# First channel product as seven half products, the second one's weights converted early and parked in device memory, and all places in the order set anew

## The chip, the cores and the metric

The kernel runs on one core of one Trainium2 chip. The metric is the device time of one execution in microseconds (us), lower is better. A core has five engines that run beside each other and meet only at semaphores: TensorE (PE in the profile, with its weight loads PEld), VectorE (DVE), ScalarE (ACT), GpSimd (POOL) and SyncE (SP), which here only issues transfers.

## The reference, cut to what matters

Three layers follow each other, for 2 batches of 448 tokens and a width of 768 (12 heads of 64):

```python
scores = cap * tanh(q @ k.T / 8 / cap)                  # attention, 24 heads
x = softmax(scores) @ v
h = gelu(x @ w_in); u, v = halves(h)                    # gated layer, 1024 wide
v_s = w_sg @ (layernorm(v) * g_ln) + b_sg
x = x + (u * v_s) @ w_out
u = x + (relu(x.T @ w_tok1) @ w_tok2).T                 # token mixing
out = u + relu(u @ w_ch1) @ w_ch2                       # channel mixing: 768 -> 1536 -> 768
```

The weights of the last two layers arrive as float64, so that each has to be narrowed to float32 on the chip. To keep float32 accuracy most products are made of three products of a high part and a rest (`hi*hi + hi*lo + lo*hi`): every operand is first split in two.

## The kernel before

Every piece of work is recorded as an operation (`Plan.op`) with the engines that could do it, a cost for each, a key and the tiles it reads and writes. `Plan.schedule` (a list scheduler in the file) then goes through time and gives each engine, among the operations whose inputs are ready and whose buffers are free, the one with the lowest key; the program is written out in the order of the planned starts. An engine runs its instructions in that order and waits where an input is not there. Buffers come from small pools by tag (`BUFS`: 20 of `a`, 13 of `h`, 6 each of `x`, `v`, `q`, 3 each of the narrowing's `r` and `t`, 4 banks `gm` and 2 double banks `sc` for the results of TensorE).

- **Attention** (`attention_all`): 12 pairs of heads. For each there are score blocks (L605, L618, into `sc`), tanh and exp on ACT (L576, L585), values (L631, L648), sums over the keys (L686) and the division (L703 to L717). A score block needs one of the two `sc` banks, which tanh frees.
- **Gated layer and token mixing**: `v_unit`, `u_unit`, `sg_unit`, `out_unit`, `tr_unit`, `tok1_unit`, `tok2_unit`. Their products are all issued in L330. `v_unit` and `u_unit` of the first batch also fill TensorE between the score blocks of the later pairs. `tok2_unit` leaves `u` as a whole tile (L1067), parks it in device memory (`kept`) and splits it (`x`).
- **First channel product, ch1** (`ch1_unit`): 12 column blocks `f`. For each there are 6 weight chunks and 3 terms over all 896 tokens: 36 products, 448 columns wide in the first two blocks, 512 and 384 in the other ten. One relu on ACT (L1098, 896 wide) drains a block into `q` or `a`.
- **Second channel product, ch2** (`ch2_all`, L1179): seven half products in place of eight. The 2 by 2 blocks of the weights (`a11` to `a22`, 128 by 384 for each of 6 `j`) and of the tokens are combined by sums. Some of these run on DVE (L1105, `change`), some as transfers that add to their target (L1160, `gather`, issued by POOL). DVE adds the results up (L1195, `onto`). Each half product is 54 products of TensorE.
- **Narrowing** (`narrow`): a raw tile `r` arrives; ACT scales it (L472) and makes two partial results (L484, L498), DVE joins them (L506). `split` then makes the high part (L417 on ACT, L418 on DVE, L422 on POOL) and the rest (L434 on DVE, L435 on POOL).

Of the kernel before, what the change touches and what calls it, by code (L numbers as in the profile page):

```python
# [18 lines left out]
DM = H * D  # L19
# [6 lines left out]
NR = 3  # L26
# [6 lines left out]
AHEAD, PACE = 62, 2.2  # L33
# [22 lines left out]
}  # L56
W_ON = {
# [17 lines left out]
    "ch2": (74, 5),  # L75
# [4 lines left out]
TURN, STAY = 200.0, 250.0  # L80
TABLE = 1290.0
EARLY = 72.0
KQ = 1.2
HALVES = ("win_u", "wsg", "wout", "tok1", "tok2", "ch1", "ch2")
# [183 lines left out]
class Net:  # L268
# [184 lines left out]
    def narrow(self, src, n, t, key, name, after=None, sign=1.0):  # L453
# [5 lines left out]
        else:  # L459
# [7 lines left out]
            if after:  # L467

                o.deps += after
            self.act(  # L470
                n,
                lambda: nc.scalar.activation(  # L472
                    raw[:, :, 1].bitcast(F32), raw[:, :, 1].bitcast(F32), AF.Copy, scale=2.0**-112
                ),
                [raw],
                [raw],
                130,
                key=key,
            )
# [181 lines left out]
    def sums(self, E, A, key, level, odd):  # L661
# [65 lines left out]
    def attention_all(self):  # L727
        xs = []
        old = None
        for n in range(B * NP + 1):  # L730
            k0 = 10.0 * n
            odd = n % 2 == 1
            if n < B * NP:
# [8 lines left out]
                for j in range(3):  # L742
                    sc = self.scores(qk, j, k0 + 0.4 * j)
                    self.weigh(sc, 2, E[j], k0 + 0.4 * j)
                if not odd:
                    sc = self.scores_rest(qks, k0 + KQ)
                    self.weigh(sc, 2, Q, k0 + KQ)
            if old:
                was = odd == 0
                oqk, oE, oA, oqks, oAs = old  # L750
                self.values(oqk, oE, oA[0], [0, 1], k0 - 2, was)
                self.values(oqk, oE, oA[0], [2], k0 + 2, was)
                if not was:
                    self.values_rest(oqks, oE[3], oAs, k0 + 2.1)
                self.sums(oE, oA[1], k0 + 2.5, LEVEL[n - 1], was)
# [302 lines left out]
    def tok2_unit(self, b, h1, w2, x2, d, kept):  # L1058
# [10 lines left out]
        u = self.x_part(d, b)  # L1069
        self.split(S, lambda: u[:, 0], lambda: u[:, 1], lambda: z.ap, [z], [u])  # L1070
        return u


    def ch1_unit(self, ws, U, f):

        nc = self.nc
        ps = self.bank2()
        even = f < 2
        for m, ts in enumerate((slice(0, S), slice(S, 2 * S)) if even else WIDE):
            terms = []  # L1080
            for d in range(ND):
# [381 lines left out]
```

## Time and profile before

| | us |
|---|---|
| median of 3 runs | 402.62 (402.31 to 403.66) |
| the profiled execution, its own time | 402.18 |
| its span from the first to the last instruction | 400.4 |
| TensorE busy within the span | 391.8 |
| VectorE, ScalarE, GpSimd busy | 292.5, 271.9, 83.9 |

The span is 1.8 us shorter than the execution's own time; that part lies around the program. TensorE's products are pipelined: a product's record lasts longer than the distance to the next one, so the work of a stage is read as the time from its first product's start to that of the next stage, divided by their number, and not as a sum of records. For DVE and ACT the busy time of a stretch divided by its count of instructions is used in the same way.

### The profile page before, as it was taken

Reading aid. Unit: us, or ns where it says so; the run is one execution under the profiler, and the core shown is the slowest. Engines: PE = TensorE matmul, PEld = TensorE weight load, DVE = VectorE, ACT = ScalarE, POOL = GpSimd, SP = SyncE. Lnnn points to the kernel's source line nnn. Section 1 sums busy time; section 2 is a strip of 40 time slices with the busy share of each in tenths; the row PEclk is TensorE's granted clock in tenths of the full one; section 3 lists DMA queues with packets and bytes.
Section 4 is the critical chain, followed back from the end, with each engine's and each line's share of the span. In section 5 each row is a group of like instructions: output and inputs, shape, how many; then the busy total and the mean of one; then the engine's idle time right before and its main releaser. Section 6 shows DMA issues by size and latency. Waiting matters only on the chain. (4 is left out here: it accounts for less than half of the span.)

```text
span 400.4 us, 5874 instructions
## 1 busy us (share of the span) xinstructions
PE 391.8 (98%) x2102; PEld 302.5 (76%) x2102; DVE 292.5 (73%) x503; ACT 271.9 (68%) x438; POOL 83.9 (21%) x96
## 2 busy tenths in 40 slices
PE   8999989999999999999999999999999999999995
PEld 4222224565567899999999998988989999999995
DVE  1799999999557869976379983435466389978871
ACT  6999999999693577365168868776667675542330
POOL 1112140000001425753000100003222141156300
PEclk9999999999999999999999999999999999999999
DMA  7975243444000114043005774558867794364112
GB/s 240 393 276 199 80 178 109 166 133 144 16 1 10 45 54 144 2 155 107 2 0 153 255 225 157 175 180 201 186 166 178 207 300 76 99 115 70 71 71 75
DMA packets 22934, 54.18 MB, mean 135 GB/s; under 512 B 2800, under 2 KB 11632, under 8 KB 22896
## 3 DMA queue, kind: packets, MB, share of 16 engines
q1 hardware_dynamic: 19008, 48.23, 37.0%
q0 software_dynamic: 3744, 5.38, 8.0%
q8 instruction: 18, 0.29, 0.3%
q14 instruction: 20, 0.16, 0.1%
q10 hardware_dynamic: 144, 0.11, 0.1%
HBM read 42.83 MB, written 5.51 MB: 121 GB/s over the span
## 5 line engine op out<-in xcount | busy, mean ns | idle before, releaser
L330 PE MATMUL sc<-x,a 128*128 128x384 f32 (+2 forms) x432 | 87.7, 364 | 0.0
L330 PEld LDWEIGHTS sc<-x,a 128*128 128x128 f32 x432 | 78.8, 188 | 8.8
L1179 PE MATMUL gm<-a,a 128*128 128x448 f32 x252 | 54.7, 367 | 0.0
L1179 PEld LDWEIGHTS gm<-a,a 128*128 128x128 f32 x252 | 47.3, 188 | 4.3
L330 PE MATMUL gm<-a,a 128*128 128x448 f32 (+1 forms) x232 | 46.3, 356 | 0.0
L472 ACT ACTIVATE r<-r 128x512 f32<-128x512 f32 (+2 forms) x64 | 40.8, 644 | 6.6 <-DMA r<-ch_in 6.5
L585 ACT ACTIVATE a<-a,acap 128x896 f32<-128x896 f32 x42 | 43.7, 1096 | 0.1
L330 PEld LDWEIGHTS gm<-a,a 128*128 128x128 f32 x232 | 42.0, 188 | 2.2
L576 ACT ACTIVATE a<-sc,qs 128x896 f32<-128x896 f32 x42 | 42.0, 1057 | 1.8 <-DVE a L667 0.9
L506 DVE SCALAR_TENSOR_TENSOR t<-r,t 128x512 int32<-128x512 int32 (+1 forms) x34 | 25.4, 753 | 23.6 <-ACT t L498 22.1
L435 POOL TENSOR_TENSOR a<-t,a 128x512 fp32r<-128x512 f32 x12 | 18.9, 1575 | 98.9 <-DVE a L418 72.1
L330 PE MATMUL gm<-q,a 128*128 128x448 f32 x160 | 33.0, 366 | 0.0
L605 PE MATMUL sc<-q 64*64 64x448 f32 x264 | 30.0, 552 | 2.2 <-ACT a L576 2.2
L330 PEld LDWEIGHTS gm<-q,a 128*128 128x128 f32 x160 | 30.0, 188 | 2.6
L631 PE MATMUL gm<-a,v 128*64 128x448 f32 x144 | 30.9, 548 | 0.0
L330 PEld LDWEIGHTS gm<-x,a 128*128 128x128 f32 x144 | 26.7, 188 | 4.9 <-DVE v L418 1.4
L330 PE MATMUL gm<-x,a 128*128 128x448 f32 x144 | 30.5, 368 | 0.0
L484 ACT ACTIVATE t<-r 128x512 uint16<-128x512 uint16 (+1 forms) x34 | 27.3, 806 | 2.7 <-DVE a L434 2.0
L1179 PE MATMUL sc<-a,a 128*128 128x448 f32 x126 | 28.9, 367 | 0.0
L656 DVE TENSOR_TENSOR a<-a,a 128x896 f32<-128x896 f32 (+1 forms) x24 | 26.9, 1122 | 1.9 <-ACT a L585 1.6
L498 ACT ACTIVATE t<-r 128x512 f16<-128x512 f32 (+1 forms) x34 | 27.1, 803 | 0.0
L330 PE MATMUL gm<-a,x 128*128 128x512 f32 x108 | 26.5, 397 | 0.0
(130 smaller groups left out, 578.8 us busy)
## 6 DMA issues: line engine op xcount, KB each, us to landing
r<-ch_in SPq DMA_DIRECT2D x18, 512.0 KB, 3.5
r<-ch_in SPq DMA_DIRECT2D x24, 384.0 KB, 3.8
r<-w_in_in SPq DMA_DIRECT2D x12, 512.0 KB, 5.1
q<-qk_in SPq DMA_DIRECT2D x11, 448.0 KB, 7.2
v<-va_in SPq DMA_DIRECT2D x12, 256.0 KB, 6.0
r<-w_out_in SPq DMA_DIRECT2D x6, 512.0 KB, 3.4
u<-h SPq DMA_DIRECT2D x12, 224.0 KB, 2.5
x<-u SPq DMA_DIRECT2D x12, 224.0 KB, 5.9
```

The costliest lines, as they stand in the source:

```text
L330: self.nc.tensor.matmul(view(), l, rr, start=(i + m == 0), stop=(i + m == n - 1))
L435: "POOL": ("POOL", n * 2.3 + 60, lambda: nc.gpsimd.tensor_tensor(**args()), True),
L472: lambda: nc.scalar.activation(raw[:, :, 1].bitcast(F32), raw[:, :, 1].bitcast(F32), AF.Copy, scale=2.0**-112),
L484: lambda: nc.scalar.activation(t.ap.bitcast(U16)[:, 0::2], raw.ap.rearrange("p n t -> p (n t)").bitcast(U16)[:, 1::4], AF.Copy, scale=2.0* ...
L498: lambda: nc.scalar.activation(t.ap.bitcast(F16)[:, 1::2], raw[:, :, 1].bitcast(F32), AF.Copy, scale=sign),
L506: lambda: nc.vector.scalar_tensor_tensor(out=t.ap.bitcast(I32), in0=raw[:, :, 1], scalar=3, in1=t.ap.bitcast(I32), op0=ALU.logical_shift_l ...
L576: lambda: nc.scalar.activation(te.ap, sc[:, 0:nn, :S], AF.Tanh, scale=self.qs),
L585: lambda: nc.scalar.activation(te.ap, te.ap, AF.Exp, scale=self.acap),
L605: nc.tensor.matmul(sc[at, h, :S], part(rows, ks), part(rows, QC), start=True, stop=True)
L631: nc.tensor.matmul(A[cols, :S], V[:, 2 * j + h], E[j][:, h], start=(j == 0 and not odd), stop=(j == 2 and odd),)
L656: "DVE": ("DVE", n / 0.96 + 70, lambda: nc.vector.tensor_tensor(**args()), True),
L1179: nc.tensor.matmul(banks[i].ap[:, :S], l, r, start=not more and (j, n) == (0, 0), stop=(j, n) == (KH - 1, 2), skip_group_check=more,)
```

## The change

1. ch1 becomes `ch1_all`, with the same scheme of seven half products as ch2. The tokens are combined once (for each of three `d` a difference, a sum, two negations and two gathers); there are 21 splits of token tiles in place of 12. For each of 6 `j` the weights come as four 128 by 384 blocks, are combined by three gathers and one sum, and give seven half products of 9 products, all 448 columns wide. Each is split on its own (42 splits of 384 columns in place of 18 of 512). Two of the seven results are drained by ACT, five by an `onto` on DVE, and three relus run on tiles outside the banks.
2. The 24 weight blocks of ch2 are narrowed before ch1 starts, written to device memory (`ahead`), and read back shortly before ch2 (`fetch`).
3. ch2's arithmetic is as before. `a21` and `a22` share tiles of the pool `a`; a gather is planned with fewer bytes.
4. All places are set anew: `off(kind, n, j)` shifts the keys of attention, normalisation, weights, ch1 and the parked blocks by a table, and a few constants change. The scheduler itself does not.

```diff
-AHEAD, PACE = 62, 2.2
+AHEAD, PACE = (36, 10), 2.2
+SCALE_ON = {"ch1": {"ACT": 0, "POOL": 200}, "ch2": {"ACT": 0, "POOL": 200}}
+CH1_ORDER = [(0, 0), (0, 1), (1, 0), (0, 2), (1, 1), (1, 2)]
+for j in range(6):
+    CH1_ORDER += [(p, j) for p in ((2, 3, 5, 4, 6) if j < 3 else (0, 2, 3, 1, 5, 4, 6))]
-    "ch2": (74, 5),
+    "ahead": (-130, 4.2),
-TURN, STAY = 200.0, 250.0
+TURN, STAY = 200.0, 267.5
-EARLY = 72.0
-KQ = 1.2
+EARLY = 72.96
+KQ = 1.42
+OFF = {
+    "a": {
+        (0, 0): 6.9, (0, 1): -3.7, (0, 2): -1.1, (1, 0): 6.2, (1, 1): 27.0, (1, 2): 12.6, (1, 3): 6.6,
...
+    "s": {
+        (0, 0): 2.0, (0, 2): 1.8, (0, 3): 4.5, (1, 0): -1.8, (1, 1): -4.1, (1, 2): 4.3, (2, 0): 5.9,
...
+def off(kind, n, j):
+    return OFF.get(kind, {}).get((n, j), 0.0)
...
-                    sc = self.scores(qk, j, k0 + 0.4 * j)
-                    self.weigh(sc, 2, E[j], k0 + 0.4 * j)
+                    at = k0 + 0.4 * j + off("s", n, j)
+                    sc = self.scores(qk, j, at)
+                    self.weigh(sc, 2, E[j], at)
...
+    def ahead(self, src, n, at, name, sign):
+        t, out = self.buf("t", [128, n]), Buf("keep", None, None)
+        out.ap = self.dram.tile([128, n], F32, tag=name, name=name, bufs=1)
+        self.narrow(src, n, t, at, "ahead", sign=sign)
+        self.load(128 * n * 4, lambda: self.nc.sync.dma_start(out=out.ap, in_=t.ap), [out], [t], key=at)
+        return out
+    def gather(self, out, a, n, at):
+        nc = self.nc
+        self.plan.op(
+            [("POOL", 1000.0, lambda: nc.gpsimd.dma_start(out=out.ap, in_=a.ap, accum_op=ALU.add), False, 0)],
+            at,
+            [a, out],
+            [out],
+            nbytes=205 * n * 4,
+        )
...
+            self.change(z11[d], z11[d], z12[d], ALU.subtract, S, lead(2, 0))
+            o22[d] = self.operand(z22[d], lead(2, 0) + 0.12)
+            self.negate(z12[d], lead(2, 0) + 0.1)
+            self.gather(z12[d], kept[1][3 + d], S, lead(2, 0) + 0.12)
+            self.change(z22[d], z22[d], z11[d], ALU.add, S, lead(2, 0) + 0.17)
...
+            product(0, j, x, a11, o11, False)
+            self.act(S, lambda x=x, o=c12: nc.scalar.copy(o.ap, x.ap[:, :S]), [x], [c12], 60, key=at[0, j])
+            product(1, j, x, a12, o21, True)
+            self.act(S, lambda x=x, o=c11: nc.scalar.activation(o.ap, x.ap[:, :S], AF.Relu), [x], [c11], 60, key=at[1, j])
+            self.gather(a11, a21, 384, at[2, j] - 18 + off("g", 0, j))
+            self.change(s2, a22, a11, ALU.add, 384, at[2, j] - 13 + off("g", 1, j))
+            product(2, j, y, s2, o2, False)
+            self.onto(c12, y, c12, at[2, j], ALU.subtract)
+            self.gather(a12, s2, 384, at[2, j] - 12 + off("g", 2, j))
+            product(3, j, z, a11, o3, False)
+            self.onto(c22, z, c12, at[3, j])
+            product(4, j, z, a22, o4, True)
+            self.onto(c21, z, c12, at[4, j])
+            self.relu(c21, at[4, j])
+            self.gather(a21, a22, 384, at[5, j] - 14 + off("g", 3, j))
+            product(5, j, v, a21, o1, False)
+            self.onto(c22, v, c22, at[5, j])
+            self.relu(c22, at[5, j])
+            product(6, j, v, a12, o22, True)
+            self.onto(c12, v, c12, at[6, j])
+            self.relu(c12, at[6, j])
...
-                narrow(t, row, col, j, k - AHEAD + (4 * j + n) * PACE)
+                self.fetch(t, f32[j, row, col], 128 * 384 * 4, k - AHEAD[n // 2] + (2 * j + n % 2) * PACE)
```

Three places show how the order moves. A row names the line, the instruction, what it writes and what it reads; `x3` means three in a row. L330, L605, L618, L631, L648, L686 and L1160 of before are L404, L675, L688, L701, L718, L756 and L1167 of the change; ch1's products stand in L1239, the POOL casts of L422 in L496.

TensorE in attention, before, at score blocks 25 to 28: `sc` are score blocks, `gm` collect values or sums, `q` holds queries and keys, `a` the exponentials, `v` the values of a pair.

```order
L631 MATMUL gm_9_468<-a_31_485,v_6_174 64x448 x2
L631 MATMUL gm_9_468<-a_32_490,v_6_174 64x448 x2
L605 MATMUL sc_25_527<-q_6_176 64x448 x4
L618 MATMUL sc_26_537<-q_6_176 64x448 x2
L618 MATMUL sc_26_537<-q_7_232 64x448 x2
L605 MATMUL sc_27_550<-q_7_232 64x448 x4
L605 MATMUL sc_28_560<-q_7_232 64x448 x4
L686 MATMUL gm_11_568<-a_30_477,ones_72 64x448 x2
```

The same score blocks of TensorE in the change.

```order
L701 MATMUL gm_10_500<-a_32_505,v_6_193 64x448 x2
L688 MATMUL sc_25_551<-q_6_195 64x448 x2
L688 MATMUL sc_25_551<-q_7_262 64x448 x2
L675 MATMUL sc_26_560<-q_5_191 64x448 x4
L701 MATMUL gm_12_571<-a_34_537,v_7_254 64x448 x2
L701 MATMUL gm_12_571<-a_35_545,v_7_254 64x448 x2
L701 MATMUL gm_12_571<-a_30_479,v_7_254 64x448 x2
L675 MATMUL sc_27_589<-q_7_262 64x448 x4
L675 MATMUL sc_28_596<-q_7_262 64x448 x4
L718 MATMUL gm_12_571<-a_36_574,v_7_254 64x448 x2
```

Before, four score blocks stand in a row, with two banks `sc`; in the change three values blocks stand between score blocks 26 and 27.

TensorE in ch1, before, in the third column block: `x_7` to `x_12` are the split tokens of both batches, `a_119` and `a_121` weights.

```order
L330 MATMUL sc_53_2368<-x_11_2168,a_121_2074 128x512 x3
L330 MATMUL sc_53_2368<-x_12_2179,a_121_2074 128x512 x3
L330 MATMUL sc_53_2368<-x_7_2110,a_119_2061 128x384 x3
L330 MATMUL sc_53_2368<-x_8_2123,a_119_2061 128x384 x3
L330 MATMUL sc_53_2368<-x_9_2129,a_119_2061 128x384 x3
```

ch1 at its start in the change: `gm_80` to `gm_82` are the banks of the first two half products, `x_10` the split tokens of the second.

```order
L1239 MATMUL gm_80_2463<-x_7_2314,a_112_2182 128x448 x3
L1239 MATMUL gm_80_2463<-x_8_2322,a_112_2182 128x448 x3
L1239 MATMUL gm_80_2463<-x_9_2351,a_112_2182 128x448 x3
L1239 MATMUL gm_81_2485<-x_7_2314,a_116_2243 128x448 x3
L1239 MATMUL gm_81_2485<-x_8_2322,a_116_2243 128x448 x3
L1239 MATMUL gm_81_2485<-x_9_2351,a_116_2243 128x448 x3
L1239 MATMUL gm_80_2463<-x_10_2355,a_118_2265 128x448 x3
```

Before, all rows write one bank `sc` and read split tokens; now nine products of 448 columns make one half product of one `j` in a bank `gm`, and the first two half products start in turn. ch1 has 378 products in place of 432.

POOL in ch1, before: the DMA rows are gathers for ch2, the TENSOR_SCALAR rows high parts.

```order
L422 TENSOR_SCALAR a_139_2717<-q_19_2377 128x448
L1160 DMA h_62_2465<-h_63_2487 128x384
L1160 DMA v_27_2549<-h_64_2604 128x384
L422 TENSOR_SCALAR a_143_2796<-q_20_2438 128x448
L1160 DMA h_64_2604<-h_65_2630 128x384
L422 TENSOR_SCALAR a_145_2836<-v_28_2713 128x384
L1160 DMA v_28_2713<-h_66_2770 128x384
```

POOL late in ch1 in the change: `h_76` to `h_79` are the four weight blocks of `j` = 4, `t_55` and `t_56` sums of blocks, `a_172` and `v_31`, `v_32` blocks of ch2.

```order
L496 TENSOR_SCALAR a_167_3096<-h_78_3069 128x384
L1167 DMA h_78_3069<-h_77_3032 128x384
L1167 DMA h_77_3032<-h_79_3101 128x384
L1167 DMA h_76_3013<-t_56_3140 128x384
L1167 DMA v_31_2521<-a_172_3150 128x384
L1167 DMA a_172_3150<-a_172_3150 128x384
L1167 DMA v_32_2575<-a_179_3238 128x384
```

There are 50 gathers in place of 26, and here six stand in a row, ch1's and ch2's behind each other.

## Rows read from the trace of the kernel before

**Rows 1.** The page's head and its first part, busy time of each engine.

```profile
span 400.4 us, 5874 instructions
PE 391.8 (98%) x2102; PEld 302.5 (76%) x2102; DVE 292.5 (73%) x503; ACT 271.9 (68%) x438; POOL 83.9 (21%) x96
```

**Rows 2.** Busy time by stretch: engine busy us (instructions), granted clock, DMA share, GB/s.

```profile
core 0: us, PE busy (x) PEld busy (x) DVE busy (x) ACT busy (x) POOL busy (x), PEclk, DMA share, GB/s
0.00:10.00 10.00, 8.56 (x50) 4.41 (x52) 1.40 (x7) 6.15 (x8) 1.23 (x10) 1.00 0.75 239
10.00:70.00 60.00, 56.98 (x387) 17.50 (x384) 56.95 (x92) 60.00 (x73) 11.51 (x8) 1.00 0.57 206
70.00:121.00 51.00, 51.00 (x293) 29.71 (x292) 39.48 (x67) 44.55 (x62) 2.28 (x4) 1.00 0.28 91
121.00:231.10 110.10, 110.10 (x567) 101.46 (x567) 87.21 (x145) 65.20 (x119) 32.91 (x28) 1.00 0.26 85
231.10:318.60 87.50, 87.50 (x433) 78.69 (x432) 45.99 (x84) 61.04 (x108) 12.96 (x17) 1.00 0.68 184
318.60:360.00 41.40, 41.40 (x203) 37.61 (x202) 35.62 (x70) 24.46 (x51) 12.55 (x16) 1.00 0.66 157
360.00:396.40 36.40, 36.26 (x179) 33.15 (x177) 25.20 (x44) 10.51 (x21) 10.45 (x14) 1.00 0.26 72
396.40:400.40 4.00, 0.00 (x0) 0.00 (x0) 0.68 (x2) 0.00 (x0) 0.00 (x0) 1.00 0.20 66
```

**Rows 3.** Waits of TensorE between 10 and 72 us: total, times, longest.

```profile
PE sc L605 <- ACT a L576: 2.2, 2, 1.8
PE sc L618 <- ACT a L576: 0.7, 1, 0.7
PE gm L686 <- DVE a L656: 0.2, 1, 0.2
```

**Rows 4.** Timeline of TensorE, 48 to 54 us: start, length, group, idle before it.

```profile
48.38 0.98 PE L605 MATMUL sc<-q 64*64 64x448 f32 x8
49.28 0.98 PE L618 MATMUL sc<-q 64*64 64x448 f32 x8
52.03 1.88 PE L605 MATMUL sc<-q 64*64 64x448 f32 x16 [1.77 <-ACT a L576]
```

**Rows 5.** Timeline of TensorE, runs of one array shape in attention.

```profile
30.49 1.72 PE L631 MATMUL gm<-a,v 128*64 128x448 f32 x8
32.14 1.80 PE L605 MATMUL sc<-q 64*64 64x448 f32 x16
...
53.84 0.97 PE L686 MATMUL gm<-a,ones 128*64 128x448 f32 x4
54.65 2.42 PE L631 MATMUL gm<-a,v 128*64 128x448 f32 x12
57.00 1.73 PE L605 MATMUL sc<-q 64*64 64x448 f32 x16
```

**Rows 6.** Groups of TensorE by shape in ch1 (count, busy us, mean ns).

```profile
L330 PE MATMUL sc<-x,a 128*128 128x512 f32 x180 | 42.8, 391 | 0.0
L330 PE MATMUL sc<-x,a 128*128 128x384 f32 x180 | 33.1, 336 | 0.0
L330 PE MATMUL sc<-x,a 128*128 128x448 f32 x72 | 15.0, 368 | 0.0
```

**Rows 7.** Products by line: duration min/median/max, first and last start.

```profile
L330 PE MATMUL sc<-x,a x432: 333/368/398, 231.1 to 318.5; 128*128 128x512 f32 x60, 128*128 128x384 f32 x60, 128*128 128x448 f32 x24
...
L1179 PE MATMUL gm<-a,a x252: 362/368/369, 319.9 to 395.9; 128*128 128x448 f32 x126
...
L1179 PE MATMUL sc<-a,a x126: 362/368/369, 318.6 to 388.6; 128*128 128x448 f32 x126
```

**Rows 8.** Gathers by line L1160 on POOL, and their time to landing.

```profile
L1160 POOL DMA_DIRECT2D v<-h x6: 862/882/1048, 271.1 to 321.2; - x6
...
DMA to landing us min/median/max: 3.0/4.4/7.2
```

**Rows 9.** POOL's costliest groups between 121 and 231.1 us.

```profile
L986 POOL TENSOR_TENSOR h<-x 128x448 f32<-128x448 f32 x12 | 17.1, 1450 | 0.6 <-DVE a L434 0.6
L435 POOL TENSOR_TENSOR a<-t,a 128x512 fp32r<-128x512 f32 x6 | 8.1, 1356 | 55.0 <-DVE a L418 41.2 <-ACT a L417 13.8
```

**Rows 10.** POOL's costliest groups between 318.6 and 360 us.

```profile
L1160 POOL DMA_DIRECT2D a<-t x6 | 5.2, 866 | 14.5 <-issue 8.7 <-DVE a L434 5.6
L1160 POOL DMA_DIRECT2D x<-x x5 | 4.4, 1197 | 7.0 <-DVE x L1195 7.0
```

More of the change, by code (lines that the diff above doesn't have):

```diff
@@ L659, in add, with sums @@
         self.plan.op([made[e] + (t,) for e, t in on.items()], key, r, w)
-    def sums(self, E, A, key, level, odd):
+    def sums(self, E, A, key, level, odd, early):
         nc = self.nc
@@ new lines, in gather, with change, onto @@
+    def gather(self, out, a, n, at):
+        nc = self.nc
+        self.plan.op(
[5 more added lines that the diff above has]
+        )
+    def change(self, out, a, b, op, n, at):
+        self.combine(n, lambda: out.ap, lambda: a.ap, lambda: b.ap, op, [a, b], [out], at, SUM_ON)
+    def onto(self, out, bank, other, at, op=ALU.add):
+        nc = self.nc
+        return self.dve(
+            S, lambda: nc.vector.tensor_tensor(out=out.ap, in0=other.ap, in1=bank.ap[:, :S], op=op), [bank, other], [out], key=at
+        )
@@ new lines, in negate @@
+    def negate(self, t, at):
+        nc = self.nc
+        made = {
+            "ACT": ("ACT", S / 1.2 + 95, lambda: nc.scalar.activation(t.ap, t.ap, AF.Copy, scale=-1.0), False),
+            "DVE": ("DVE", S / 1.92 + 70, lambda: nc.vector.tensor_scalar(t.ap, t.ap, -1.0, None, ALU.mult), True),
+            "POOL": ("POOL", S * 0.84 + 160, lambda: nc.gpsimd.tensor_scalar(t.ap, t.ap, -1.0, None, ALU.mult), True),
+        }
+        self.plan.op([made[e] + (n,) for e, n in NEG_ON.items()], at, [t], [t])
@@ L1191, in banks @@
             return [Part(self.bank2(), lambda ap: ap[:, 0]), self.bank(), last or self.bank()]
-        def onto(out, bank, other, at, op=ALU.add):
-            return self.dve(
-                S, lambda: nc.vector.tensor_tensor(out=out.ap, in0=other.ap, in1=bank.ap[:, :S], op=op), [bank, other], [out], key=at
-            )
         def store(o, m, b, at):
@@ L1240, in ch2_all @@
         for i in three:
-            onto(part[3 + i], z[i], part[i], key(4, 0, 4))
+            self.onto(part[3 + i], z[i], part[i], key(4, 0, 4))
             u = U[0][3 + i]
-            gather(u, part[i], S, key(4, 0))
+            self.gather(u, part[i], S, key(4, 0))
         for j in js:
@@ L1273, in ch2_all @@
             u = U[1][3 + i]
-            last = onto(u, v[i], u, key(6, 0, 4))
+            last = self.onto(u, v[i], u, key(6, 0, 4))
             store(u, 3 + i, 1, key(6, 0))
@@ L1308, in run @@
         late = None if self.anycap else 1
-        vn[0] = stage([lambda s=s: self.v_unit(x[0], win_v, s, late) for s in range(NR)], 6.5)
-        u[0] = stage([lambda f=f: self.u_unit(x[0], win_u, f, late) for f in range(NF)], 6.5)
+        vn[0] = stage([lambda s=s: self.v_unit(x[0], win_v, s, late) for s in range(NR)], 6.5, "a", 0)
+        u[0] = stage([lambda f=f: self.u_unit(x[0], win_u, f, late) for f in range(NF)], 6.5, "a", 1)
         k = early
@@ L1315, in run @@
             u[0] = [f() for f in u[0]]
-        vn[1] = stage([lambda s=s: self.v_unit(x[1], win_v, s) for s in range(NR)], 4)
+        vn[1] = stage([lambda s=s: self.v_unit(x[1], win_v, s) for s in range(NR)], 4, "a", 2)
         self.key = k
```

269 lines of the change are left out of this document (168 added, 101 removed), and 20 rows, old and new, of the table OFF.

## The prediction

> **What bounds the kernel now.** The first view is the busy time of the engines over the span: TensorE 391.8 of 400.4 us, VectorE 73%, ScalarE 68%, GpSimd 21% [rows 1]. Those shares are means, so the second view is the busy time by stretch [rows 2]. The granted clock is 1.00 in every stretch, so the clock is no term below. From 70.0 to 396.4 us TensorE has 0.14 us without work. Between 10 and 70 us it lacks 3.02 of 60.00 us, and there ScalarE is busy for all 60.00. The third view, TensorE's waits, names most of these 3 us: score blocks that wait for tanh of ScalarE to free one of two banks (2.2 and 0.7 us) [rows 3], the longest of them 1.77 us at 52.03, just the place of the first fence of the part on the change [rows 4]. So the kernel is as long as TensorE's row of products, with some 3 us of holes in attention; a change is worth what it takes out of that row, less the holes that it makes.
>
> **The base.** The profiled execution takes 402.18 us, 400.4 of span and 1.78 around it; it lies 0.44 below the median of 402.62. Terms below are added to 402.18, and the result is used for the median unchanged, since 0.44 is 0.1%. A measurement of this kernel can tell about 0.3% (1.2 us) from no change.
>
> **ch1, 432 products to 378.** ch1's products start at 231.1 and ch2's at 318.6 [rows 7]: 87.5 us, all of it TensorE's [rows 2]. The changed ch1 has ch2's very shape, 128 by 128 weights and 448 columns in a bank, so I price it at ch2's pace: from 318.6 to the last start at 395.9 there are 377 distances, 77.3/377 = 0.205 us each. 378 products by 0.205 are 77.5 us, **10.0 less**. Two bounds: the 72 products of 448 columns that ch1 has now took 15.0 us [rows 6], 0.208 each, so 78.7 us and −8.8; and by columns, of which ch1 streams 193,536 now (432 by 448 on the mean) and 169,344 then, 0.875 of 87.5 is 76.6 us and −10.9. I keep ch2's pace, for it is that of the same shape in the same scheme. The bound by columns is the far one: records of 384 columns took 336 ns and of 512 took 391 [rows 6], so the time doesn't fall in step with the columns.
>
> **Attention's turns of shape.** Places set anew change how often TensorE turns from score blocks (64 by 64) to values, sums and wide products. Counted in the order there are 48 runs of one shape before and 41 after. A turn has a price: four sums and 12 values of one shape, 16 records, go from 53.84 to 57.00, 3.16 us, and 8 values go from 30.49 to 32.14, 1.65 us [rows 5]. The 8 more records are (3.16 − 1.65)/8 = 0.189 each, so 1.65 − 8 by 0.189 leaves 0.14 us for the run's turn. Seven fewer: **−1.0**; 0 if they stood only where TensorE waits anyway.
>
> **Attention's holes.** Four score blocks in a row with two banks made the wait of 1.77 us; in the change three values blocks stand in that row, 6 records by 0.189, 1.1 us of cover. ScalarE stays full there whatever the order is, and other rows may bunch instead. Bounds: all holes go (−3.0), or another wait like the longest is added (+1.8). I take **−0.8**, some three quarters of the 1.1 us that the three blocks cover.
>
> Without a new stall the sum is 402.18 − 10.0 − 1.0 − 0.8 = **390.4 us**. The rest asks what comes late now.
>
> **The feeders as a whole.** The change adds combining sums, negations, splits and additions from the banks: counted in the order VectorE has 584 instructions for 503, ScalarE 516 for 438, GpSimd 50 gathers for 26, SyncE 186 issues for 132. A pace is the busy time of a stretch over its instructions [rows 2]. New ch1: VectorE 120 by 0.5475 (45.99/84) = 65.7 us and ScalarE 112 by 0.565 = 63.3, beside 75.6 us of TensorE (the 369 products from ch1's first to the first of ch2). Between the last attention sum and ch1: 189 ScalarE instructions by 0.548 = 103.6, 171 of VectorE by 0.601 = 102.9, beside 603 products by 0.194 (110.1/567) = 117. ch2: VectorE 130 by 0.5335 (60.82/114) = 69.4 beside 79.3. On the mean of each stage TensorE stays the bound, with some 10 us to spare in each; before, the spare in ch1 was 41.5. So the early narrowing of ch2's weights (24 blocks, three ScalarE instructions and one join each) costs nothing on the path: it moves into 121 to 231 us, where ScalarE is busy for 65.20 of 110.1 us. If that cover went, the price would be at most what ScalarE lacks, which at 103.6 of 117 is none.
>
> **VectorE's densest stretch.** A mean can hide a dense place. In the changed order it is from the drain of bank `gm_97`, late in ch1, to the one at `sc_59` in ch2: 90 VectorE instructions against 234 products, 48.0 us at 0.205. At the pace of 318.6 to 360 us (35.62/70 = 0.509) they take 45.8 us and are hidden; at ch1's pace (0.5475) 49.3, 1.3 too long; at 0.601, the pace of 121 to 231 us [rows 2], 54.1, 6.1 too long. The last is the stretch where GpSimd runs additions of two inputs, 1,450 and 1,356 ns each [rows 9], but it also holds 512-wide joins. In the dense stretch of the change GpSimd holds 21 gathers and 2 casts, as it does in ch2 now [rows 10]. So I take the middle pace, **+1.3**, with 0 and +6.1 as the ends.
>
> The Trainium skill, "SBUF — State Buffer", section "Who interferes with whom", states that a VectorE instruction with two inputs in SBUF contends with a GpSimd instruction that reads SBUF, and that whoever comes second blocks. The slower pace beside GpSimd's additions [rows 9] agrees with it; gathers that carry only descriptors would by it leave VectorE at 0.509, and the term +1.3 would be 0.
>
> **The gathers.** Each is issued by GpSimd and landed 3.0, 4.4 and 7.2 us later (shortest, median, longest) [rows 8]. Its lead is the number of products between its place and its first reader's, by 0.205. The shortest lead before was 71 products, 14.6 us. In the change six are under 7.2 us: 17, 27, 28, 29, 32 and 34 products, so 3.5, 5.5, 5.7, 5.9, 6.6 and 7.0 us, all for ch1's weights of the late `j`, where the second fence of GpSimd shows six gathers in a row. A gather here is followed by a sum or by a split, then by products, so a late one stops TensorE. At the median landing one is late, 4.4 − 3.5 = **+0.9**; if all land at 7.2 the six lack 9.0 together. Below 0 it can't go, as nothing is taken from the path.
>
> By the Trainium skill, "DMA: Bandwidth & Descriptors", section "Anatomy of one DMA — SWDGE (gpsimd) path", such a transfer takes 2.0 us and its bytes over 436 GB/s, an estimate of 2.45 us for 196,608 bytes; the sum would then be 392.1, without the 0.9. The median of 4.4 us [rows 8] differs, and the measurement decides.
>
> **The start of ch1.** The first two half products read tokens that are only split, not combined, but their weights go through a narrowing and a split that compete with 24 early blocks on ScalarE and VectorE, and the transfers for parking (24 blocks of 192 KB written, and read back later) come into stretches with a DMA share of 0.26 and 0.68 [rows 2]. In ch2 now the hole at the start is none (41.40 busy of 41.40 us) [rows 2]; for a bank or a block late by one VectorE instruction or so I take **+0.4**, with 0 and +1.8 (the longest wait of the trace [rows 4]) as ends.
>
> Sum: 390.4 + 1.3 + 0.9 + 0.4 = **393.0 us**, 2.3% less.
>
> **The rivals.** *VectorE takes over as bound around the turn from ch1 to ch2.* For it: the spare falls to 10 us a stage, five of seven results now need VectorE, and a bank that isn't drained stops TensorE. Against it: ch2 already runs 70 VectorE instructions over 203 products without a hole. Price at pace 0.601: 390.4 + 6.1 + 0.9 + 0.4 = 397.8 us.
>
> *The gathers land late* (the slower side). The place is late ch1; 50 gathers go through GpSimd in place of 26, one behind the other, beside parked blocks that are read back over the same DMA engines, whose share in ch1 is 0.68 already. Were landings twice the median, 8.8 us, eight gathers would be late (two more with leads of 7.4 and 8.2) by 20.6 us in all: 390.4 + 20.6 = 411 us. From a mean landing of 7.8 us on the lateness reaches 13 us and the kernel is slower than before. Against it: the longest of the six in the row was 7.2, and a wait of TensorE gives later gathers lead back, so this is an upper price.
>
> *The new places lose in attention.* ScalarE is full there, and a second wait of 1.8 us, no saving on turns and none on holes gives 392.2 + 1.8 + 2.6 (the three small stalls) = 396.6 us.
>
> *No new stall and all holes gone*: 402.18 − 10.0 − 1.0 − 3.0 = 388.2 us.
>
> *The change doesn't do what it says*: 378 products are in the order, so the product count can't fail; only the pace can, which its bounds hold.
>
> **How the numbers follow.** Forecast 393.0: 0.60. VectorE as bound 397.8: 0.20. New places lose, 396.6: 0.06. No stall, 388.2: 0.08. Late gathers, 411: 0.06. The range takes the forecast with its bounds (390.4 less a little of the −10.9 bound, 389.5) up to VectorE's and attention's rivals and a us more, 399.0; left out are the best case, the late gathers and a little of the first two, 0.2 in all. Faster by over 0.3%: all but the late gathers and a small part of what mixes with them, 0.90; within 0.3%: 0.03; slower: 0.07.
>
> **What would show it.** Right: ch1's first product to ch2's first about 76 us with TensorE busy throughout; TensorE's clock at 1.00; waits of TensorE on ScalarE's tanh under 3 us. Each stall has its own releaser: TensorE waiting for `onto` or a rest on VectorE late in ch1 (VectorE's rival), VectorE waiting for a gather's landing (late gathers, landings above 7 us), TensorE waiting for tanh (attention). The forecast is wrong if the pace of 448-column products in ch1 is not near 0.205, or if stalls after 231 us exceed 8 us.

## The result

| | before | changed |
|---|---|---|
| median (us) | 403.07 (402.31 to 403.66, 4 runs) | 398.80 (396.95 to 399.54, 4 runs) |
| profiled execution, its span | 402.18, 400.4 | 396.95, 395.2 |
| ch1's first product starts at | 231.1 | 236.6 |
| from there to the span's end | 169.3 | 158.6 |

The ratio is 0.9886, with an interval of 0.9862 to 0.9911: the change saves 1.1%, where 2.3% were forecast. The time lies inside the range, near its upper end, but the change gives 4.3 us where more than 9 were forecast. Nothing is lost where the forecast looked for it: from ch1's first product on the kernel is 10.7 us shorter. The loss lies ahead of ch1, which now starts 5.5 us later. The profiled execution is the shortest of the four; in a second profile of the same kernel (e1) ch1 starts at 237.3 and the part behind is 8.5 us shorter than before.

The page's head and first part for the changed kernel, which answer to [rows 1].

```profile
span 395.2 us, 6055 instructions
PE 381.3 (97%) x2048; PEld 296.7 (75%) x2048; DVE 327.8 (83%) x584; ACT 295.5 (75%) x516; POOL 105.8 (27%) x117
```

Busy time by stretch, as in [rows 2] and with the same columns, with cuts at the changed kernel's own stages (ch1 from 236.6, ch2 from 312.1).

```profile
core 0: us, PE busy (x) PEld busy (x) DVE busy (x) ACT busy (x) POOL busy (x), PEclk, DMA share, GB/s
0.00:10.00 10.00, 7.78 (x42) 3.98 (x44) 1.20 (x8) 5.73 (x8) 1.22 (x10) 1.00 0.77 241
10.00:70.00 60.00, 56.82 (x395) 18.73 (x395) 56.81 (x88) 59.58 (x70) 9.20 (x7) 1.00 0.54 188
70.00:121.00 51.00, 51.00 (x295) 30.24 (x295) 47.20 (x85) 49.52 (x78) 2.84 (x5) 1.00 0.41 126
121.00:236.60 115.60, 112.07 (x566) 102.07 (x565) 94.72 (x157) 88.98 (x172) 41.27 (x37) 0.99 0.62 192
236.60:312.10 75.50, 75.13 (x371) 69.21 (x370) 60.68 (x120) 53.25 (x113) 23.91 (x28) 1.00 0.81 200
312.10:390.50 78.40, 78.40 (x388) 72.45 (x386) 66.47 (x129) 38.45 (x80) 27.36 (x32) 1.00 0.62 139
```

TensorE's waits in the whole span of the changed kernel (total us, times, longest), beside those of [rows 3], which go from 10 to 72 us.

```profile
PE gm L404 <- ACT a L491: 3.3, 1, 3.3
PE gm L701 <- ACT a L655: 1.5, 2, 1.2
PE gm L756 <- DVE a L726: 1.1, 1, 1.1
PE sc L675 <- ACT a L646: 1.0, 2, 0.8
...
PE gm L1239 <- DVE x L508: 0.4, 1, 0.4
```

The reader is to see three things. ch1 and ch2 together have holes of 0.37 us. Attention has about the holes that it had (60.00 − 56.82 = 3.18 us for 3.02). The stretch between, where TensorE was busy for all 110.1 us before, now has 3.53 us of holes, 3.3 of them one wait, and a mean granted clock of 0.99. The clock in finer steps around that wait (columns: busy TensorE, granted clock, DMA share, GB/s):

```profile
178.00:179.00 1.00, 0.00 (x0) 1.00 0.45 164
...
180.50:181.00 0.50, 0.50 (x2) 0.59 0.84 342
181.00:181.50 0.50, 0.50 (x3) 0.50 0.87 193
...
183.50:184.00 0.50, 0.50 (x3) 0.50 1.03 243
184.00:185.00 1.00, 1.00 (x7) 1.00 0.81 237
```

TensorE stands still from 177 to 180.4 us, and from 180.6 to 184 us its granted clock is 0.50, the lower level of 1.2 GHz. That is seven steps of half a microsecond, one of them at 0.59: 0.5 by (0.41 + 6 by 0.50) = 1.7 us lost. So up to ch1 the account is: holes 8.93 us where there were 4.46 (up to 10, 70 and 236.6 us: 2.22 + 3.18 + 3.53), +4.5; the clock, +1.7; the rest, −0.7, which fewer turns may have given; together the 5.5 us.

### The profile page after: what moved, and what is told of

Same layout as the page of the kernel before. It is cut to its first block, busy times and chain, and to the rows that moved or that the text cites. A ratio compares the mean times of both kernels' runs of the same rounds, so it can differ in the third digit from the quotient of the medians.

```text
span 395.2 us, 6055 instructions
## 1 busy us (share of the span) xinstructions
PE 381.3 (97%) x2048; PEld 296.7 (75%) x2048; DVE 327.8 (83%) x584; ACT 295.5 (75%) x516; POOL 105.8 (27%) x117
## 5 line engine op out<-in xcount | busy, mean ns | idle before, releaser
L404 PE MATMUL gm<-a,a 128*128 128x448 f32 (+1 forms) x232 | 48.6, 366 | 3.5 <-ACT a L491 3.3
L404 PEld LDWEIGHTS gm<-a,a 128*128 128x128 f32 x232 | 42.9, 193 | 7.3 <-ACT a L491 4.0
L655 ACT ACTIVATE a<-a,acap 128x896 f32<-128x896 f32 x42 | 42.5, 1054 | 0.0
L546 ACT ACTIVATE r<-r 128x384 f32<-128x384 f32 (+1 forms) x65 | 38.6, 597 | 3.3 <-DMA r<-ch_in 2.3
L491 ACT CAST a<-h 128x384 fp32r<-128x384 f32 (+3 forms) x51 | 27.3, 541 | 14.5 <-DVE h L1035 7.4
L508 DVE TENSOR_TENSOR a<-h,a 128x384 fp32r<-128x384 f32 (+3 forms) x56 | 35.1, 634 | 3.7 <-ACT a L491 3.5
L1239 PE MATMUL gm<-x,a 128*128 128x448 f32 x162 | 35.5, 366 | 0.4 <-DVE x L508 0.4
L404 PE MATMUL gm<-q,a 128*128 128x448 f32 x160 | 33.4, 366 | 0.0
L1239 PEld LDWEIGHTS gm<-x,a 128*128 128x128 f32 x162 | 30.3, 188 | 3.2 <-DVE x L508 0.7
L701 PE MATMUL gm<-a,v 128*64 128x448 f32 x144 | 31.1, 548 | 1.5 <-ACT a L655 1.5
L404 PEld LDWEIGHTS gm<-q,a 128*128 128x128 f32 x160 | 30.0, 188 | 2.6
L675 PE MATMUL sc<-q 64*64 64x448 f32 x264 | 29.6, 549 | 1.0 <-ACT a L646 1.0
L404 PE MATMUL gm<-x,a 128*128 128x448 f32 x144 | 30.6, 367 | 0.0
L404 PEld LDWEIGHTS gm<-x,a 128*128 128x128 f32 x144 | 26.8, 188 | 4.2 <-DVE h L787 0.7
L576 DVE SCALAR_TENSOR_TENSOR t<-r,t 128x384 int32<-128x384 int32 (+2 forms) x40 | 27.9, 700 | 1.8 <-ACT t L568 1.5
L509 POOL TENSOR_TENSOR a<-t,a 128x512 fp32r<-128x512 f32 x8 | 11.9, 1491 | 63.0 <-DVE a L492 42.1
L554 ACT ACTIVATE t<-r 128x384 uint16<-128x384 uint16 (+2 forms) x40 | 27.9, 698 | 0.0
```

What stands on the lines that cost most here:

```text
L404: self.nc.tensor.matmul(view(), l, rr, start=(i + m == 0), stop=(i + m == n - 1))
L508: "DVE": ("DVE", n / 0.96 + 70, lambda: nc.vector.tensor_tensor(**args()), not psum),
L546: "ACT": ("ACT", n / 1.2 + 130, lambda: nc.scalar.activation(high(), high(), AF.Copy, scale=2.0**-112), False),
L554: lambda: nc.scalar.activation(t.ap.bitcast(U16)[:, 0::2], raw.ap.rearrange("p n t -> p (n t)").bitcast(U16)[:, 1::4], AF.Copy, scale=2.0* ...
L576: lambda: nc.vector.scalar_tensor_tensor(out=t.ap.bitcast(I32), in0=raw[:, :, 1], scalar=3, in1=t.ap.bitcast(I32), op0=ALU.logical_shift_l ...
L655: lambda: nc.scalar.activation(te.ap, te.ap, AF.Exp, scale=self.acap),
```

## What the hole is made of

The timeline of the changed kernel ahead of the hole (start, length, group, idle before it).

```profile
165.49 13.13 POOL L1058 TENSOR_TENSOR h<-x 128x448 f32<-128x448 f32 x9
...
174.64 1.57 DVE L1035 TENSOR_TENSOR h<-h,h 128x448 f32<-128x448 f32 x1
174.76 0.79 ACT L554 ACTIVATE t<-r 128x512 uint16<-128x512 uint16 x1
...
176.13 1.50 DVE L576 SCALAR_TENSOR_TENSOR t<-r,t 128x384 int32<-128x384 int32 x1
...
178.10 1.01 DVE L508 TENSOR_TENSOR a<-h,a 128x448 fp32r<-128x448 f32 x1
...
179.03 0.68 DVE L576 SCALAR_TENSOR_TENSOR t<-r,t 128x512 int32<-128x512 int32 x1
...
179.75 0.62 ACT L491 CAST a<-t 128x512 fp32r<-128x512 f32 x1 [0.31 <-DVE t L576]
...
180.42 6.80 PE L404 MATMUL gm<-a,a 128*128 128x448 f32 x24 [3.35 <-ACT a L491]
```

TensorE waits for the high part of a `w_out` block (512 wide). ScalarE makes it as soon as VectorE has joined the block (L576, 179.03). ScalarE had its two partial results ready at about 177.5 us, but VectorE was late: ahead of that join stand an instruction of the gated layer, an early join of ch2 (384 wide) and a rest, and they take 1.57, 1.50 and 1.01 us (one more, L1050, takes 0.61). GpSimd runs additions of two tiles beside them (`whole`, L1058: the residual's high part plus its rest), nine in a row from 165.5 to 178.6 us. VectorE's groups in that time (count, busy us, mean ns):

```profile
L508 DVE TENSOR_TENSOR a<-h,a 128x448 fp32r<-128x448 f32 x3 | 3.4, 1120 | 0.2 <-ACT a L491 0.2
L576 DVE SCALAR_TENSOR_TENSOR t<-r,t 128x384 int32<-128x384 int32 x2 | 3.2, 1577 | 0.0
L1035 DVE TENSOR_TENSOR h<-h,h 128x448 f32<-128x448 f32 x2 | 3.1, 1570 | 0.0
L576 DVE SCALAR_TENSOR_TENSOR t<-r,t 128x512 int32<-128x512 int32 x1 | 1.6, 1647 | 0.0
L1029 DVE SCALAR_TENSOR_TENSOR h<-gm,gln,bsg 128x448 f32<-128x448 f32 x2 | 1.3, 669 | 0.0
L1050 DVE TENSOR_TENSOR h<-gm,h 128x448 f32<-128x448 f32 x2 | 1.2, 612 | 0.0
L508 DVE TENSOR_TENSOR a<-t,a 128x512 fp32r<-128x512 f32 x1 | 0.8, 819 | 0.7 <-ACT a L491 0.7
```

Instructions with two inputs in SBUF (`h`, `a`, `t` and `r` tiles) take 0.82 to 1.65 us each; those with one input in a bank (`gm`) keep their 0.61 and 0.67. Eight instructions of the first kind start while an addition of GpSimd's runs, and each ends 0.4 to 0.55 us after that addition has ended: for the last three the additions end at 175.73, 177.22 and 178.63 us, and the instructions at 176.21, 177.63 and 179.11. So the engines do not meet only at semaphores, as the first section has it. **Theory A** is this collision: GpSimd's additions hold VectorE up just where the early narrowing has brought it more work. **Rival B**: VectorE has too many instructions there, whatever GpSimd does. **Rival C**: ScalarE's own row is late, with three more instructions for each block narrowed early.

## The experiments

The kernel before ran beside each group, with medians from 402.37 to 402.97. Three runs each take one suspect away, beside a second run of the changed kernel.

**The changed kernel again.**

> The changed kernel once more, beside the three runs below. In its trace TensorE waits 3.3 us at 177 to 180.4 us (products of L404 for a high part of L491), and then its granted clock is 0.50 from 180.5 to 184 us. If this hole is a steady part of the kernel, it stands here too, within 1 us of that place, the granted clock dips behind it, and the median is near 398.8 us. If it was an accident of one execution, it is missing here or stands elsewhere.

399.15 us (397.87 to 399.92), ratio 0.9909 (0.9882 to 0.9935). The hole stands at the same place with 3.4 us, the clock dips behind it, and ch1 starts at 237.3. It is a steady part of the kernel.

**Without GpSimd's additions.**

```diff
-            lambda: self.nc.gpsimd.tensor_tensor(out=out.ap, in0=parts(0), in1=parts(1), op=ALU.add),
+            lambda: self.nc.sync.dma_start(out=out.ap, in_=parts(0)),
```

> The changed kernel with the 12 additions of GpSimd in `whole` (L1058) taken out: each is replaced by a transfer that copies the high part only, so the rest of x is left out of the residual. The order of everything else is kept. Theory A (GpSimd's nine additions in a row, 165.5 to 178.6 us, hold up the two-input instructions of VectorE beside them, 851 against 672 ns for a sum, 894 against 604 for a join): the hole of 3.3 us and the dip of the clock (3.4 us at half speed, 1.7 us lost) go, ch1 starts at about 231.6 in place of 236.6, and the median is 398.8 - 5.0 = 393.8 us. Rival B (VectorE simply has too many instructions there, since the 24 joins of the early narrowing came in): a hole of 2 us or more stays, 396.5 to 399. Rival C (ScalarE's own row is late, by the three instructions a block of the early narrowing): no change, 398.8.

393.61 us (392.33 to 394.41), ratio 0.9770 (0.9750 to 0.9791). The hole and the dip are gone, and ch1 starts at 230.2. Theory A gave the size.

**The additions on VectorE.** In the same line `gpsimd` becomes `vector`.

> The changed kernel with the 12 additions of `whole` issued by VectorE in place of GpSimd, at the same places of the order; the result is the same. Theory A: VectorE gets 12 by 0.62 = 7.4 us more work, 5.6 us of it in the place of the nine in a row, but its other instructions there go back to 0.55 to 0.7 us (some 15 of them lose 0.3 to 1.0 us each now); the hole shrinks below 1.5 us and the clock stays up, 394 to 396 us. Rival B: 5.6 us more for an engine that is the bound there, the hole grows from 3.3 to some 7 to 9 us, 402 to 405 us. Rival C: little change, 397.5 to 399.5 us.

393.43 us (392.57 to 395.39), ratio 0.9793 (0.9764 to 0.9821), with nothing left out. VectorE gets 12 instructions more, and the hole, which should grow by Rival B, is gone. The stretch in both kernels, the changed one first:

```profile
160.00:170.00 10.00, 10.00 (x51) 9.26 (x51) 9.99 (x15) 6.53 (x11) 5.98 (x5) 1.00 0.65 203
170.00:180.00 10.00, 6.89 (x32) 5.44 (x30) 9.10 (x11) 6.80 (x14) 8.63 (x6) 1.00 0.27 75
```

```profile
160.00:170.00 10.00, 10.00 (x51) 9.27 (x50) 9.79 (x19) 8.38 (x17) 2.00 (x1) 1.00 0.64 193
170.00:180.00 10.00, 10.00 (x51) 9.27 (x50) 9.20 (x18) 8.59 (x19) 0.00 (x0) 1.00 0.67 208
```

In the same 20 us VectorE (third pair) is as busy, 18.99 for 19.09 us, but gets 37 instructions done in place of 26. The groups of VectorE between 150 and 178 us with the additions on it:

```profile
L1058 DVE TENSOR_TENSOR h<-x 128x448 f32<-128x448 f32 x10 | 6.1, 617 | 0.0
...
L1035 DVE TENSOR_TENSOR h<-h,h 128x448 f32<-128x448 f32 x7 | 4.3, 616 | 0.0
...
L576 DVE SCALAR_TENSOR_TENSOR t<-r,t 128x384 int32<-128x384 int32 x4 | 2.2, 548 | 0.0
```

An addition costs GpSimd 1.5 us and VectorE 0.62 us. The Trainium skill, "SBUF — State Buffer", section "Who interferes with whom", says that two SBUF inputs on VectorE contend with a GpSimd instruction that reads SBUF, and that the later one blocks. The runs agree, with 616 against 1,570 ns for L1035 and no change for inputs in a bank, and the ends of the eight instructions above fit a block that lasts until the addition is over.

**Without the early joins.**

```diff
-                    lambda: nc.vector.scalar_tensor_tensor(
+                    lambda: None if name == "ahead" else nc.vector.scalar_tensor_tensor(
```

> The changed kernel without the 24 joins on VectorE of the early narrowing (the low bits of ch2's weights are left out); ScalarE's instructions for it, the parking and GpSimd's additions stay, the order too. Three of these joins stand between 150 and 178 us and take 1.55 us each there, 4.7 us in all. Theories A and B: the hole of 3.3 us goes, since VectorE gets 4.7 us free ahead of it, the clock stays up, 393 to 395 us. Rival C (ScalarE): the hole stays, 398 to 399 us.

394.16 us (392.51 to 394.86), ratio 0.9781 (0.9754 to 0.9808), no hole, ch1 at 232.0. ScalarE's instructions are all there, so Rival C falls. Either half of the collision is enough to remove it: it needs the additions and the early joins together.

**The kernel before without GpSimd's additions** (the edit of e2, in L986).

> The kernel before with the 12 additions of GpSimd in `whole` (L986) taken out in the same way (a transfer copies the high part, the rest of x is left out of the residual). There the adds stand in runs of four, three, three and two with pauses between them, and TensorE has no hole in that stretch. Theory A (the adds cost something only where VectorE has no time to spare): no change, 402.4 within 0.6 us. Rival (they cost TensorE time wherever they stand, in ways that the waits don't show): 397 to 400 us.

403.20 us, ratio 1.0009 (0.9995 to 1.0024). The additions cost the kernel before nothing; no early joins stand between them there.

**Which part of the change made the collision?** Two kernels without any of the new places (`off` returns 0, the three constants as before), one with the additions on VectorE, the other on GpSimd as in the change.

```diff
...
-    return OFF.get(kind, {}).get((n, j), 0.0)
+    return 0.0
```

> The kernel of e3 (393.43 us) with no shift at all (the whole table off) and TURN/STAY, EARLY and KQ as before the change: ch1's new scheme and the early narrowing without the new places. Theory (the new places carry a good part: e7's attention alone was worth 6 us with what came behind it): 400 to 408 us. Rival (ch1's fewer products carry it all, the places only settle details): 393 to 396 us.

> As e10 (no shift at all, 394.75 us), but with the additions of `whole` on GpSimd as in the change, so that only the new places differ from the changed kernel. GpSimd's row then has ten of these additions behind each other, between products 345 and 323 ahead of ch1 (the change: nine, between 333 and 322). Theory 1 (the collision comes from the early narrowing, whose instructions meet the additions whatever the places are): a hole before the products of w_out or w_tok of 2 us or more, a dip of the clock behind it, 397.5 to 401 us. Theory 2 (the new places made the collision): no hole there, 394 to 395.5 us.

With the additions on VectorE 394.75 us (ratio 0.9802, 0.9781 to 0.9822); on GpSimd 404.95 us (1.0043, 1.0026 to 1.0060). So the second is 10 us slower by that one engine. Two waits of TensorE and GpSimd's row in it:

```profile
PE gm L404 <- DVE a L492: 7.0, 1, 7.0
...
PE gm L404 <- DVE a L508: 0.9, 1, 0.9
```

```profile
167.97 14.31 POOL L1058 TENSOR_TENSOR h<-x 128x448 f32<-128x448 f32 x10
```

Ten additions in a row, a hole of 7.0 us, and then 180 to 190 us at a mean clock of 0.57 (the profiled execution is the longest of five, 408.83 us). Theory 2 falls and Theory 1 was too mild: the early narrowing makes the collision, and the new places lessen it (404.95 to 398.80). Once the collision is gone the new places are worth 1.3 us by the medians (394.75 to 393.43), and 0.4 by the ratios to the kernel before (0.9802 and 0.9793), whose intervals overlap. So no gain of theirs is shown there, where I expected 6 us or more.

**The clock apart from the hole.** Sixteen products, whose results are overwritten, ahead of the product that waits.

```diff
...
+                for _ in range(16):
+                    nc.tensor.matmul(ps[:, :S], wout[3][:, 0, 0:128], g[0][:, 0], start=True, stop=True)
...
```

> The changed kernel (398.8 and 399.15 us) with 16 more products of TensorE, whose results are overwritten, right ahead of the product that waits 3.3 us for the high part of a w_out block at 177 to 180.4 us (gm_52, fifth row of the first batch); they read tiles that are there, so TensorE works through the hole, 16 by 0.205 = 3.3 us. Theory (the granted clock falls to 0.50 for 3.4 us because TensorE stood still before it): the clock stays at 1.00 there, and the time falls by half of 3.4 us, 1.7 us, to 397.1 us within 0.7, though TensorE does more work. Rival (the clock falls for another reason at that place, or the hole is not where the time goes): the dip stays and the time is 398.8 to 399.5 us; if the products don't fit into the hole, up to 401.

398.22 us (397.62 to 400.38), ratio 0.9891 (0.9867 to 0.9914). TensorE's timeline:

```profile
174.92 2.33 PE L404 MATMUL gm<-a,a 128*128 128x448 f32 x10 [0.18 <-DVE a L508]
177.09 3.47 PE L1052 MATMUL gm<-a,a 128*128 128x448 f32 x16
180.62 7.60 PE L404 MATMUL gm<-a,a 128*128 128x448 f32 x34
```

The products fill the hole, the dip behind it is gone, and ch1 starts at 235.5, 1.1 us ahead of the changed kernel's first profile and 1.8 ahead of its second, around the 1.7 expected. The mean granted clock of the whole execution is 0.997 to 1.000 in all six runs, and 0.991 to 0.996 in the eight of the changed kernel. So the clock fell because TensorE stood still. In the median 0.6 to 0.9 us of it are seen, not clear of the spread, and 398.22 is above the 397.1 within 0.7 that I gave; the section on the hardware shows what may hide the rest.

**The gathers on VectorE.** In `gather`, for ch1's weights (on top of e3):

```diff
...
+            add = lambda: nc.vector.tensor_tensor(out=out.ap, in0=out.ap, in1=a.ap, op=ALU.add)
...
```

> The changed kernel with the additions of `whole` on VectorE (393.43 us) and, beside that, the 24 gathers of weights in ch1 issued as additions on VectorE, in place. Up to 99 VectorE instructions now stand beside 234 products (48.0 us), where 92 did. Theory of the forecast (VectorE's dense stretch has little to spare, the paces measured in the changed ch1 and ch2 are 0.506 and 0.515 us): 99 by 0.51 = 50.5 us, some 2.5 us too long, and a second dense place at ch1's start (32 against 60 products, 16.3 us against 12.3) makes a hole of its own: 396 to 401 us. Rival (landings of gathers are what delays ch1; in place there is no landing): 392 to 393.5 us.

395.10 us, ratio 0.9802 (0.9777 to 0.9828). That is 1.7 us over e3 by the medians, 0.4 by the ratios, whose intervals overlap, and below the 396 to 401 that I gave. No hole came in the dense place late in ch1: between 261 and 312 us TensorE is busy for 50.98 of 51.00 us. At ch1's start, between 231 and 261, it lacks 2.43 us, where e3 lacks 1.68; behind that, up to 300 us, it runs ch1 at the slower of the two paces of the last section. So the dense place had more to spare than the forecast's term says.

**Attention's old places** (shifts of scores, values, sums and divisions off, the constants back, on top of e3).

> The kernel of e3 (393.43 us) with attention's places as before the change: no shifts for scores, values, sums, their order and the division, and the three constants TURN/STAY, EARLY and KQ back. TensorE turns its shape 10 times more often (52 runs against 42). Theory (a turn costs 0.14 us and the holes for tanh come back): 10 by 0.14 = 1.4 us and up to 2 us of holes, 394.5 to 397 us, with the time up to the last attention sum that much longer. Rival (ScalarE is full in attention and sets its end whatever the order): 393 to 394 us.

399.80 us (397.65 to 402.50), ratio 0.9928 (0.9899 to 0.9958). ch1 starts at 233.0, 2.2 us later than in e3, with as many holes up to there (5.53 for 5.50 us): by that the ten turns cost 0.22 us each, where the forecast had 0.14. But e3 and e4, with one order of TensorE, differ there as well: e4 starts ch1 at 232.0 with 5.94 us of holes, 0.8 us later beyond what its holes explain. So the price of a turn stays open. The holes did not come back: attention has 2.06 us of them between 10 and 70 us, and e3 3.19. The rest of the 6 us comes behind: from ch1's first product to ch2's last it takes 158.7 us where e3 takes 155.3, with stops between 244 and 257 and between 291 and 298 us. That half of the table doesn't fit without the other half may be the cause; no run shows it. e10, with none of the table, is faster. Such a run undoes more than it names.

**Without early narrowing and parking** (on top of e3).

```diff
...
-                self.fetch(t, f32[j, row, col], 128 * 384 * 4, k - AHEAD[n // 2] + (2 * j + n % 2) * PACE)
+                self.narrow(f32[j, row, col], 384, t, k - AHEAD[n // 2] + (2 * j + n % 2) * PACE, "ch2", sign=(1.0, -1.0)[col])
...
```

> The kernel of e3 (393.43 us) without early narrowing and parking: ch2's 24 weight blocks are narrowed where they were read back. The order around is worked out again. Theory by the mean (ch1 then has 136 VectorE instructions by 0.506 = 68.8 us, ch2 144 by 0.515 = 74.2, both under TensorE's 75.5 and 78.4; ScalarE less): no cost, and the stretch before ch1 is relieved, 392 to 394 us. Theory by the dense place (103 VectorE instructions against 234 products, 48.0 us; 103 by 0.515 = 53.0): holes of about 5 us in late ch1 and early ch2, 396 to 400 us.

411.95 us, ratio 1.0201 (1.0154 to 1.0248). Both theories were too mild, and the one by the mean is off by 18 us. The longest groups of TensorE's waits:

```profile
PE gm L1239 <- ACT a L491: 2.7, 2, 1.6
PE sc L1350 <- DVE a L508: 2.5, 2, 2.3
PE sc L1239 <- ACT a L491: 2.4, 1, 2.4
PE sc L1350 <- ACT a L491: 1.8, 2, 1.6
```

From 231 to 411 us TensorE is busy for 163.03 of 180 us, VectorE for 142.31 and ScalarE for 120.28: neither of the two is full, and yet TensorE lacks 12.5 us up to the end of its last product at 406.55, spread over many places, with dips of the clock. In this order new ch1 needs the early narrowing; without it the seven half products are no gain at all.

**The additions by transfers.** SyncE copies the high part, a transfer of GpSimd's adds the rest.

```diff
...
+                self.nc.sync.dma_start(out=out.ap, in_=parts(0)),
+                self.nc.gpsimd.dma_start(out=out.ap, in_=parts(1), accum_op=ALU.add),
...
```

> The changed kernel with each of the 12 additions of `whole` made by two transfers (SyncE copies the high part, GpSimd issues a transfer that adds the rest); the result is the same and no engine adds. Theory (what slows VectorE is GpSimd's own addition over its tiles, and issuing a transfer does not): as without the additions (393.61) or a little less, 392.5 to 394 us, VectorE's joins near 0.60 us there. Rival (any work of GpSimd beside VectorE slows it, issues too, or the landings of 3 to 13 us come late for the drains): 396 to 400 us.

401.68 us (398.02 to 403.93), ratio 0.9957 (0.9927 to 0.9988). TensorE waits 4.6 us at 180 to 190 us, but now GpSimd's queue stands for the copies' landing (15.1 us of waits from 168 to 192 us) and the drains for the additions' (4.4 us), while the DMA share there is 1.02 to 1.08. The rival's mechanism of late landings held, at more than its 396 to 400 us. Issues alone do not slow VectorE: beside them, between 150 and 192 us, a 384-wide join takes 0.55 us and L1035 0.62. The two slow ones, L1035 at 155.62 with 3.09 us and a join at 164.99 with 1.78, run beside an instruction of GpSimd's that makes a rest (L509).

The lowest median is that of e3, 393.43 us; those of e2, e4, e6 and e10 lie within its spread.

## Why the prediction was wrong

**The feeders as a whole: the step that failed.** It took 117 us of products between attention and ch1, set 102.9 us of VectorE and 103.6 of ScalarE against them, and wrote that the moved narrowing costs nothing. If that cover went, it priced what ScalarE lacks, which is none; the engine that came to lack time is VectorE. Both are means over 110 us. The stretch has a dense place: in the kernel before, too, VectorE (third pair) was busy for 9.86 and 9.83 of 10 us in 150 to 160 and 160 to 170 us, beside the additions of [rows 9].

```profile
150.00:160.00 10.00, 10.00 (x51) 9.27 (x50) 9.86 (x14) 7.89 (x15) 5.40 (x4) 1.00 0.48 144
160.00:170.00 10.00, 10.00 (x51) 9.27 (x50) 9.83 (x13) 3.16 (x7) 8.02 (x6) 1.00 0.01 2
```

In the changed kernel two of the early joins are put just there, at 157.0 and 164.3 us, and a third at 176.1. Cost: 3.3 us of hole and 1.7 of clock, which e2, e3 and e4 give back. I did look for VectorE's densest stretch, but by the number of its instructions, and took the one late in ch1. The rule on two inputs and the additions of 1,450 ns were both in the prediction, as the price of a rival in late ch1, where GpSimd only issues gathers, and not where the additions run. A rival with the right mechanism stood at the wrong place; that its price of 397.8 us is near the measured 398.80 is luck.

**The price of a hole.** The bounds for new waits were lengths of waits. Behind this one the clock ran at half for 3.4 us, half as much again. The longest wait before, 1.77 us [rows 4], had no such dip behind it, and the prediction took the clock for no term.

**ch1's products, right.** ch1's first to ch2's first product is 75.5 us (77.0 in e1) where about 76 were forecast, and 87.5 before. The pace of 0.205 that prices it is itself the mean of two, as the last section shows. The lines' records, which answer to [rows 7]:

```profile
L1239 PE MATMUL gm<-x,a x162: 362/365/468, 236.6 to 308.2; 128*128 128x448 f32 x162
...
L1350 PE MATMUL sc<-a,a x126: 362/365/369, 312.1 to 383.0; 128*128 128x448 f32 x126
```

**The three small stalls, too large.** VectorE's dense stretch, the gathers and ch1's start were to cost 1.3 + 0.9 + 0.4 = 2.6 us; all holes from 236.6 us on are 0.4. In the second profile of the same kernel (e1) they are 1.6, and in e3 1.7; there TensorE waits at ch1's start for ScalarE to drain the first half product, in e1 as

```profile
PE gm L1239 <- ACT q L1268: 1.2, 1, 1.2
```

So the term for ch1's start (+0.4, at most +1.8) was too small in some executions, and the other two were nothing. VectorE's pace there was 60.68/120 = 0.506 and 66.47/129 = 0.515 us, near the lowest of the paces offered. The gathers landed, shortest, median and longest, as

```profile
DMA to landing us min/median/max: 3.0/4.9/14.7
```

against [rows 8]. The longest are those of a burst, nine issued between 244 and 251 us that land one after another; the ones with short leads late in ch1 landed soon enough, and TensorE never waited for one.

**Attention.** Turns were to bring −1.0 and holes −0.8. What a turn costs stays open (e7), and the holes did not shrink: up to 70 us they grew from 4.46 to 5.40. In e3, where nothing else disturbs the stretch, ch1 starts at 230.8, 0.3 us earlier than before, where 1.8 were forecast.

Without the collision the kernel takes 393.43 us beside the forecast 393.0. That is in part chance: in e3's profile ch1 starts 1.5 us later than forecast, and the part from there on is 2.0 us shorter than forecast (159.9 us for 169.3 − 10.0 + 2.6 = 161.9). But the one wrong step has about the size of the gap.

## What to carry to other kernels

Before work is moved into a stretch because its engines are idle there on the mean, cut the stretch into tens of microseconds and look for the place where the receiving engine is full already. Where GpSimd adds or combines tiles, price VectorE's instructions with two inputs in SBUF beside it at up to three times their own time, and ask first whether VectorE can't do that addition itself in less. A hole of TensorE costs more than its length when the clock falls behind it.

## What the runs showed of the hardware

One thing was not expected. The same products of 448 columns run at either of two steady paces at a granted clock of 1.00. Read from the starts of successive products, they come 207, 207 and 206 ns apart (mean 206.7), or 202, 203, 202, 199 and 207 in turn (mean 202.7), and one pace lasts for tens of microseconds. The records differ too, e2 and e3 in ch2:

```profile
L1350 PE MATMUL gm<-a,a x252: 367/368/368, 308.3 to 387.4; 128*128 128x448 f32 x126
```

```profile
L1350 PE MATMUL gm<-a,a x252: 362/365/369, 309.1 to 386.1; 128*128 128x448 f32 x126
```

The same products take 79.1 us in one and 77.0 in the other; 0.6 us of the difference is one stop of e2's at 353 us. e2 and e9 ran ch1, and most or all of ch2, at the slower pace, the profiles of the changed kernel, e1 and e3 at the faster one; the kernel before changed within ch2, at 363 us. Over the 756 products of ch1 and ch2 the two differ by 756 by 4.0 ns = 3.0 us. That is as much as several of the terms above, and may be why e9's median moved less than its stage: its profile takes 156.5 us from ch1's first product to ch2's last, the changed kernel's first 153.7. What chooses the pace is open: it often changes at a short hole, but at 363 us in the kernel before there was none.
